# Moving the loads of q, k and v to ScalarE's queue, and dense instead of padded one-hot rows, in a fused attention and channel-mix kernel

## The chip, the cores and the metric

The kernel runs on one core of one Trainium2 chip. The metric is device microseconds of one execution. The engines are named as in the profile: PE is TensorE (with PEld, its weight loads), DVE is VectorE, ACT is ScalarE, POOL is GpSimd and SP is SyncE. A "q" after a name (SPq, ACTq) means the engine's sequencer, which also issues DMA transfers.

## The reference

Four batches, eight heads, 768 positions and a head dimension of 64. Queries and keys are assigned to the nearest of 16 centroids of their head, by the cosine. A query attends only to keys with the same centroid. The attention output, with the heads side by side (512 columns), goes through a channel mix with a shift by one position.

```python
q_assign = argmax(einsum('bhsd,hcd->bhsc', q_n, c_n))      # the same for k
mask = q_assign[:, :, :, None] == k_assign[:, :, None, :]
scores = where(mask, scale * (q @ k.T), -1e9)
x = softmax(scores) @ v                                    # heads side by side: (4, 768, 512)
xk = mu_k * x + (1 - mu_k) * x_prev                        # xr in the same way with mu_r
k = relu(xk @ w_k);  v = (k * k) @ w_v                     # 512 -> 1024 -> 512
out = sigmoid(xr @ w_r) * v
```

## The kernel before

**Pairs and steps.** Two heads make a pair; there are 16 pairs, n = 0 to 15. A pair takes 12 steps, one per head and block of 128 keys, so pair n begins at step s = 12n and there are 192 steps. In step t, `scores(t)` has PE multiply 128 keys with all 768 queries of the head (L281, L282) into a PSUM tile `st`, of which there are two, and ACT makes `pt`, the exp (L284). `values(t - 6)`, next on PE, multiplies six `pt` tiles of the head before with `vt` (L294). For the first block of queries of a head, at a step T that is a multiple of 6, the last of these six tiles is the exp of step T-1.

**The mask.** The score contraction has 80 rows: 64 of q or k, and 16 of a one-hot of the centroid. Both lie in `aug`, of which there are three rings of two tiles, `augs[n % 3]`. Equal centroids add a constant that the exp takes off again with its bias; without it the exp is close to zero.

**Preparation of pair n+2, during pair n.** `qk_nat` (or `qk_rows` for pairs 0 to 5; two buffers together) receives q and k from memory. The DVE transposes them into `qkT` in four calls (`trans`, L139; for the pairs up to 5 PE transposes them, `trans_pe`, L155, and DVE or ACT copies). POOL casts `qkT` into `aug` (L169). PE multiplies with the centroids (`aff_mm`, L188), DVE transposes the product to `t` (L192), takes the maximum over 16 (L199), compares (`ohn`, L202) and transposes the one-hot back to `oht` (L211). Then four transfers, issued on SP's queue, bring the one-hot rows from `oht` to rows 64 to 79 of `aug` (L213, `aff_back`). Before the change `ohn` has 32 columns for each row of the one-hot, 16 of them zero, and both halves of a group lie side by side in `oht`: 768 columns, and one transfer per group.

**Loads.** `load_rows` (L85) brings q and k of a pair in two transfers of 384 KB; `load_qk` (L78), for pairs 6 to 15, in eight of 96 KB; `load_v` (L99) brings v, cast by `vcast` on POOL (L176). Nearly all are issued on SP's queue.

**The order.** It is written out by hand. `at(t, f)` puts f at the end of step t; `forced[t]` puts it after `values`. In the other steps a slice of the channel mix (`psk`, `psr`, `psv`) is taken from a queue. These slices share two PSUM tiles, and end in ACT (`kr`, L378; `tanh`, L388) and DVE (`k`, L379; `out_sb`, L400). Every engine and every queue works in the order in which its instructions were written:

```python
at(s + 9 + i, load_qk, n + 4, i // 4, i % 4)      # n >= 4, i = 0..7
at(s + 6 + d, aff_back, n + 2, [nc.sync])         # d = 9, 5, 3, 3 for n = 0..3, then 1
at(s + 8, load_v, n + 2, nc.sync)
```

**Semaphores of the transfers.** Transfers issued from SP and from ACT share eight completion semaphores in the built program. A transfer whose semaphore was used before waits for the landing of the transfer that used it last; which one that is follows from the order of all transfers, of both queues. In the kernel before, 194 of these 197 transfers are issued from SP; the other three are ACT's, at the start.

Of the kernel before, what the change touches and what calls it, by code (L numbers as in the profile page):

```python
# [9 lines left out]
BF16 = mybir.dt.bfloat16  # L10
AF = mybir.ActivationFunctionType
ALU = mybir.AluOpType
# [4 lines left out]
def kernel(  # L17
# [13 lines left out]
    nc = tc.nc  # L31

    B, H, S, D = q.shape
    C = centroids.shape[1]
    NCH = S // 128
    NP = H // 2
# [6 lines left out]
    GW = 2 * S // NG  # L43
# [9 lines left out]
    constp = ctx.enter_context(tc.tile_pool(name="constp", bufs=1))  # L53
# [3 lines left out]
    clup = ctx.enter_context(tc.tile_pool(name="clup", bufs=2))  # L57
# [12 lines left out]
    nat = {}  # L70
    vnat = {}

    def load_qk(n, i, a):
        b, j = divmod(n, NP)
        if i == 0 and a == 0:
            nat[n] = loadp.tile([128, 2, 2 * GW], F32, name="qk_nat")
        x = (q, k)[i][b, 2 * j:2 * j + 2].rearrange("h (m i r) (w e) -> r w i (h m) e", i=32, r=2, e=32)
        nc.sync.dma_start(nat[n][32 * a:32 * a + 32, i, :].rearrange("i (m e) -> i m e", e=32),  # L78
                          x[a // 2, a % 2])

    def load_rows(n, eng_q, eng_k):
# [24 lines left out]
    mu_k_sb = constp.tile([128, NJ], F32)  # L106
    mu_r_sb = constp.tile([128, NJ], F32)
# [4 lines left out]

    NR = 3
    vts, augs, xts = [], [], []
    ohns = [constp.tile([128, 2 * GW], BF16, name=f"ohn{i}") for i in range(2)]
    for i in range(NR):
        vts.append(constp.tile([128, 2, NCH, D + 2], BF16, name=f"vt{i}"))
        augs.append([constp.tile([128, 2 * S], BF16, name=f"aug{i}_{t}") for t in range(2)])
        xts.append(constp.tile([128, S + 2], BF16, name=f"xt{i}"))

    def init_ring(i):
        if i < 2:
            nc.gpsimd.memset(ohns[i], 0.0)
        nc.gpsimd.memset(vts[i][:, :, :, D:D + 1], 1.0)
        nc.gpsimd.memset(xts[i][:, GW:GW + 2], 0.0)

# [4 lines left out]
    def augv(n, g):  # L131
        return augs[n % NR][g % 2].rearrange("p (q r u) -> p q r u", q=2, r=2)[:, g // 2, :, :]
# [46 lines left out]
    aff = {}  # L179

    def aff_mm(n, part=0, parts=1):
        j = n % NP
        if part == 0:
            aff[n] = ps_w.tile([128, GW], F32, name="affps", tag="w")
        ps = aff[n]
        u = slice(part * GW // parts, (part + 1) * GW // parts)
        for g in range(NG):
            nc.tensor.matmul(ps[32 * g:32 * g + 32, u], cblk[:, 2 * j + g % 2, :, :], qkT[n][:, g, u],  # L188
                             start=True, stop=True, tile_position=(0, 32 * g))
        if part == parts - 1:  # L190
            t1 = clup.tile([128, GW], F32, name="t1")
            nc.vector.transpose(t1, ps)  # L192
            aff[n] = t1

    def aff_max(n):
        t1 = aff[n]
        rmax = clup.tile([128, GW // C], F32, name="rmax")
        t1v = t1.rearrange("p (g c) -> p g c", c=C)
        nc.vector.tensor_reduce(rmax, t1v, axis=AX.X, op=ALU.max)  # L199

        ohn = ohns[n % 2]
        nc.vector.tensor_tensor(  # L202
            ohn.rearrange("p (r b c) -> p b r c", r=2, c=2 * C)[:, :, :, 0:C],
            t1.rearrange("p (b r c) -> p b r c", r=2, c=C),
            rmax.rearrange("p (b r) -> p b r", r=2)[:, :, :, None].to_broadcast([128, GW // (2 * C), 2, C]),
            op=ALU.is_ge)

    def aff_back(n, engs):
        aff.pop(n)
        oht = clup.tile([128, 2 * GW], BF16, name="oht")  # L210
        nc.vector.transpose(oht, ohns[n % 2])  # L211
        for i, g in enumerate((0, 2, 1, 3)):
            engs[i % len(engs)].dma_start(augs[n % NR][g % 2][64:64 + C, (g // 2) * S:(g // 2 + 1) * S],  # L213
                                          oht[32 * g:32 * g + C, :])

# [200 lines left out]
    def at(t, fn, *args):  # L418
        todo.setdefault(t, []).append(lambda: fn(*args))

    with tc.manual_schedule():
# [8 lines left out]
        load_v(0, nc.sync)  # L430
        make_identity(nc, ident)
        init_ring(0)
        nc.gpsimd.tensor_copy(identb, ident)
        def use_pe(m):
# [32 lines left out]
        for i in range(1, NR):  # L467
            init_ring(i)
# [3 lines left out]
        def more(n, i, m, eng=None, pool=None):  # L472
            for i in range(i, i + m):
                trans_pe(n, i, eng or nc.vector, pool)

        def load_mu():
            nc.sync.dma_start(mu_k_sb, moe_mu_k.rearrange("(j p) -> p j", p=128))
            nc.sync.dma_start(mu_r_sb, moe_mu_r.rearrange("(j p) -> p j", p=128))

        def load_wk(j):  # L480
            nc.gpsimd.dma_start(w_k_sb[:, j, :], moe_w_k.rearrange("(j p) f -> p j f", p=128)[:, j, :])
# [13 lines left out]
        def less_one():  # L495
            for m in (mu_k_sb, mu_r_sb):
                nc.vector.tensor_scalar(m, in0=m, scalar1=-1.0, scalar2=None, op0=ALU.add)

        at(6, load_mu)
        at(17, less_one)  # L500
        for i in range(4):
# [13 lines left out]
            3: lambda: aff_mm(1),  # L515
            4: lambda: first_onehot(1),
        }
        at(3, load_rows, 3, nc.sync, nc.sync)
        at(4, aff_max, 1)
        at(4, aff_back, 1, [nc.sync])  # L520
        for n in range(NPAIR):
            s = n * W
            off = (6, 2, 0, 0)[n] if n < NP else 0
            if n + 4 < NPAIR:
                if n + 4 < NP + 2:
                    at(s + off + 6, load_rows, n + 4, nc.sync, nc.sync)
                elif n < NP:
                    for i in range(8):
                        at(s + 6 + i // 2, load_qk, n + 4, i // 4, i % 4)
                else:  # L530
                    for i in range(8):
                        at(s + 9 + i, load_qk, n + 4, i // 4, i % 4)
            if n + 2 < NPAIR:
                if n < NP:
                    for i in range(6):
                        forced[s + i + off] = lambda n=n, i=i: more(n + 2, 2 * i, 2, nc.scalar if i == 3 else nc.vector)
                    a = (12, 8, 6, 6)[n]
                    for i in range(2):
                        forced[s + a + i] = lambda n=n, i=i: aff_mm(n + 2, i, 2)
                    d = a - 3  # L540
                else:
                    for g in range(4):
                        at(s + g, trans, n + 2, g)
                    forced[s + 5] = lambda n=n: aff_mm(n + 2)
                    d = 1
                at(s + 5 + d, aff_max, n + 2)
                at(s + 6 + d, aff_back, n + 2, [nc.sync])
                at(s + 8, load_v, n + 2, nc.sync)
            if n + 1 < NPAIR:
                at(s + 7, vcast, n + 1)  # L550
            at(s + W - 1, norm, 2 * n)
            e = s + W + NCH
            at(e - 1, norm, 2 * n + 1)
            if n < NP - 1:
                for i in range(3):
                    at(e + (4 if n == 0 else 2) + i, xtr, n, i, 3)
                e += 6 if n == 0 else 4
            else:
                at(e + 1, xtr, n)

            def sh(n=n):
                b, j = divmod(n, NP)
                if j == 0:
                    mixes[b] = Mix(b)
                mixes[b].shift(n)

            def sh2(n=n):
                b, j = divmod(n, NP)
                mixes[b].shift_r(n)

            def enq(n=n):
                b = n // NP
                queue.extend(mixes[b].slices())
                rate[0] = len(queue) / (H * NCH) if b < B - 2 else (len(queue) - HOLD) / (H * NCH - NCH - 4)
                credit[0] = 0.0
            at(e + 2, sh)
            at(e + (4 if n < NP - 1 else 3), sh2)
            if n % NP == NP - 1:
                at(e + 3, enq)
# [46 lines left out]
```

## Time and profile before

| what | value |
|---|---|
| time, median of 3 runs | 267.85 us (264.1 to 269.74) |
| the profiled execution: its time, its span | 267.85 us, 266.1 us |
| PE busy | 252.7 us |
| ACT busy | 192.3 us |
| DVE busy | 179.9 us |
| POOL busy | 100.6 us |
| mean granted PE clock | 0.987 |
| DMA | 29.71 MB, 112 GB/s in the mean |

In the lines of the profile that follow, a group is given as: source line, engine, operation, output <- input, count, busy time and the mean duration of one. A timeline row begins with the start in us and the duration in us; "xN" means that N instructions were merged, and the square bracket tells how long the engine was idle before and what ended that. A waits row gives: who waited, for whom, the total in us, how often, the longest.

### The profile page before, as it was taken

The page shows a single profiled execution, that of the slowest core. Times are in us where ns is not written, and L with a number is a line of the kernel's source. Part 1 is how long each engine was busy: PE and PEld are TensorE (multiplying, and loading weights), DVE is VectorE, ACT ScalarE, POOL GpSimd, SP SyncE. Part 2 cuts the span into 40 slices and gives each one's busy share as a digit, 9 for nine tenths or more (in the row PEclk, how much of TensorE's full clock was granted, in tenths as well). Part 3 has the DMA queues.
Part 4 walks back from the last instruction along what each step waited for, and adds up shares of the span by engine and source line. Part 5 has one row for each costly group of instructions (what it writes and reads, how often), then busy time and mean ns, then how long its engine had stood idle before and what let it go on. Part 6 is the DMA issues. An engine that isn't in the chain of part 4 may idle for free.

```text
span 266.1 us, 6335 instructions
## 1 busy us (share of the span) xinstructions
PE 252.7 (95%) x2460; PEld 153.3 (58%) x2460; DVE 179.9 (68%) x346; ACT 192.3 (72%) x275; POOL 100.6 (38%) x193
## 2 busy tenths in 40 slices
PE   8798998998899999999999999999999999999994
PEld 3666666664466655555666555555666655555441
DVE  3245769869888877685879685868887364675222
ACT  4149887988688977677889878776989887446310
POOL 3744775586998252507070525233240100000000
PEclk9869999999999999999999999999999999999999
DMA  6823788989288463929390918576302011120132
GB/s 183 246 70 109 160 198 197 182 137 190 25 163 125 111 85 94 179 69 200 81 201 15 173 15 188 119 134 142 115 0 76 1 53 68 42 79 2 39 118 79
DMA packets 93517, 29.71 MB, mean 112 GB/s; under 512 B 65904, under 2 KB 89904, under 8 KB 93488
## 3 DMA queue, kind: packets, MB, share of 16 engines
q1 hardware_dynamic: 90336, 26.26, 45.4%
q0 software_dynamic: 2208, 2.62, 6.6%
q10 hardware_dynamic: 944, 0.43, 0.6%
q8 instruction: 19, 0.31, 0.5%
q14 instruction: 10, 0.08, 0.1%
HBM read 24.15 MB, written 6.29 MB: 114 GB/s over the span
## 4 chain that ended last, share of the span: by engine, by line
PE 78%; DVE 9%; ACT 8%; DMA 2%; issue 1%; ACTq 0%; DVEq 0%
PE psv L396 16%; PE st L281 12%; PE psk L373 10%; PE out L294 10%; PE psr L385 8%; ACT pt L284 6%; PE st L282 6%; PE affps L188 5%; PE psk L364 5%; DMA qk_rows<-in_k_dram 2%; PE trps L155 2%; PE xtps L321 1%; DVE oht L211 1%; PE aff L243 1%; DVE xk L349 1%
## 5 line engine op out<-in xcount | busy, mean ns | idle before, releaser
L284 ACT ACTIVATE pt<-st 128x768 bf16<-128x768 f32 x192 | 148.4, 811 | 33.3 <-PE st L282 32.7
L169 POOL TENSOR_SCALAR aug<-qkT 64x384 bf16<-64x384 f32 x128 | 68.3, 534 | 93.7 <-DVE qkT L139 37.2
L294 PEld LDWEIGHTS <-pt 128*128 128x128 bf16 x1152 | 60.4, 97 | 28.3 <-ACT pt L284 3.3
L281 PE MATMUL st<-aug 80*128 80x512 bf16 x192 | 73.9, 385 | 1.9 <-ACT pt L284 0.7
L294 PE MATMUL out<-vt,pt 128*128 128x65 bf16 x1152 | 67.4, 193 | 1.9 <-ACT pt L284 1.3
L282 PE MATMUL st<-aug 80*128 80x256 bf16 x192 | 52.4, 273 | 0.0
L396 PE MATMUL psv<-w_v_sb,k 128*128 128x512 bf16 x192 | 47.9, 378 | 0.2 <-ACT tanh L388 0.2
L378 ACT ACTIVATE kr<-psk 128x512 bf16<-128x512 f32 x48 | 28.7, 598 | 10.7 <-PE psk L373 7.6
L379 DVE TENSOR_TENSOR k<-kr 128x512 bf16<-128x512 bf16 x48 | 23.1, 481 | 18.1 <-ACT kr L378 18.1
L373 PE MATMUL psk<-xk,w_k_sb 128*128 128x512 bf16 x128 | 32.5, 378 | 0.9 <-DVE xk L349 0.9
L400 DVE SCALAR_TENSOR_TENSOR out_sb<-tanh,psv 128x512 f32<-128x512 bf16 x24 | 16.5, 686 | 24.6 <-PE psv L396 24.5
L281 PEld LDWEIGHTS <-aug 80*128 80x128 bf16 x192 | 19.0, 99 | 18.9 <-issue 10.6
L388 ACT ACTIVATE tanh<-psr 128x512 bf16<-128x512 f32 x24 | 14.3, 597 | 15.8 <-PE psr L385 15.2
L396 PEld LDWEIGHTS <-k 128*128 128x128 bf16 x192 | 16.4, 97 | 15.7 <-issue 1.6
L282 PEld LDWEIGHTS <-aug 80*128 80x128 bf16 x192 | 19.0, 99 | 10.8 <-issue 2.6
L385 PE MATMUL psr<-w_r_sb,xr 128*128 128x512 bf16 x96 | 24.6, 378 | 0.0
L176 POOL CAST vt<-v_nat 128x384 bf16<-128x384 f32 x32 | 17.3, 568 | 12.3 <-DMA v_nat<-in_v_dram 11.5
L139 DVE STREAM_TRANSPOSE qkT<-qk_nat 128x384 f32<-128x384 f32 x40 | 20.9, 554 | 0.0
L192 DVE STREAM_TRANSPOSE t<-affps 128x384 f32<-128x384 f32 x15 | 8.7, 583 | 17.6 <-PE affps L188 17.5
L307 DVE TENSOR_TENSOR xn<-out,rs 128x384 bf16<-128x384 f32 x32 | 17.8, 558 | 1.1
L188 PE MATMUL affps<-qkT,cblk 128*32 128x384 f32 (+1 forms) x152 | 17.7, 431 | 0.8 <-DVE qkT L139 0.6
L349 DVE SCALAR_TENSOR_TENSOR xk<-diff,mu_k_sb,xt 128x768 bf16<-128x768 bf16 x16 | 16.7, 1041 | 0.6
(63 smaller groups left out, 220.3 us busy)
## 6 DMA issues: line engine op xcount, KB each, us to landing
v_nat<-in_v_dram SPq DMA_DIRECT2D x16, 384.0 KB, 4.1
out_dram<-out_sb SPq DMA_DIRECT2D x24, 256.0 KB, 2.0
qk_nat<-in_q_dram SPq DMA_DIRECT2D x40, 96.0 KB, 4.0
qk_nat<-in_k_dram SPq DMA_DIRECT2D x40, 96.0 KB, 3.7
qk_rows<-in_q_dram SPq DMA_DIRECT2D x5, 384.0 KB, 4.1
qk_rows<-in_k_dram SPq DMA_DIRECT2D x5, 384.0 KB, 5.0
aug<-oht SPq DMA_DIRECT2D x60, 24.0 KB, 2.2
w_k_sb<-in_moe_w_k_dram POOLq DMA_DIRECT2D x4, 256.0 KB, 5.0
```

The source lines that it names most:

```text
L139: nc.vector.transpose(qkT[n][:, g, :], nat[n][:, g // 2, (g % 2) * GW:(g % 2 + 1) * GW])
L169: nc.gpsimd.tensor_scalar(augv(n, g)[0:64, par, :], in0=qkT[n][64 * par:64 * par + 64, g, :], scalar1=qk_scale, scalar2=1.0, op0=ALU.mult, ...
L188: nc.tensor.matmul(ps[32 * g:32 * g + 32, u], cblk[:, 2 * j + g % 2, :, :], qkT[n][:, g, u], start=True, stop=True, tile_position=(0, 32 * g))
L281: nc.tensor.matmul(st[:, 0:512], kc, a[rows, 0:512], start=True, stop=True)
L282: nc.tensor.matmul(st[:, 512:S], kc, a[rows, 512:S], start=True, stop=True)
L284: nc.scalar.activation(pt, st, AF.Exp, bias=-BIG, scale=BIG)
L294: nc.tensor.matmul(o[:, qc, :], pts[bh * NCH + c][:, qc * 128:(qc + 1) * 128], vts[n % NR][:, tt, 2 * (c % 3) + c // 3, 0:D + 1], start=(c ...
L373: nc.tensor.matmul(ps, w_k_sb[:, j, ii * 128:(ii + 1) * 128], self.xk[:, j, 0:512], start=(j == 0), stop=(j == NJ - 1))
L378: nc.scalar.activation(kr, src, AF.Relu)
L379: nc.vector.tensor_tensor(dst, kr, kr, op=ALU.mult)
L385: nc.tensor.matmul(ps, self.xr[:, j, sl], w_r_sb[:, j, :], start=(j == 0), stop=(j == NJ - 1))
L396: nc.tensor.matmul(self.psvt, self.k2[:, i, sl], w_v_sb[:, i, :], start=(i == 0), stop=(i == NI - 1))
```

## The change

There are three parts. First, the one-hot is compared into a dense tile of 384 columns and transposed so; since the two halves of a group then lie below each other, on 16 partitions each, eight transfers of 12 KB per pair take the place of four of 24 KB. The two constant `ohn` tiles and their memsets go. Second, loads of q, k, v and of `mu_k`, `mu_r` in the steps are issued on ACT's queue, except q of pair 3; those of the start stay where they were. SP's queue keeps the one-hot transfers and the stores. Third, loads move: `load_rows` two steps later, `load_qk` to one per step from step s+8, `load_v` two steps earlier.

```diff
-    def load_qk(n, i, a):
+    def load_qk(n, i, a, eng):
...
-        nc.sync.dma_start(nat[n][32 * a:32 * a + 32, i, :].rearrange("i (m e) -> i m e", e=32),
+        eng.dma_start(nat[n][32 * a:32 * a + 32, i, :].rearrange("i (m e) -> i m e", e=32),
...
-    ohns = [constp.tile([128, 2 * GW], BF16, name=f"ohn{i}") for i in range(2)]
...
-        if i < 2:
-            nc.gpsimd.memset(ohns[i], 0.0)
...
-        ohn = ohns[n % 2]
-        nc.vector.tensor_tensor(
-            ohn.rearrange("p (r b c) -> p b r c", r=2, c=2 * C)[:, :, :, 0:C],
-            t1.rearrange("p (b r c) -> p b r c", r=2, c=C),
-            rmax.rearrange("p (b r) -> p b r", r=2)[:, :, :, None].to_broadcast([128, GW // (2 * C), 2, C]),
-            op=ALU.is_ge)
+        ohn = clup.tile([128, GW], BF16, name="ohn")
+        nc.vector.tensor_tensor(ohn.rearrange("p (g c) -> p g c", c=C), t1v,
+                                rmax[:, :, None].to_broadcast([128, GW // C, C]), op=ALU.is_ge)
+        aff[n] = ohn
...
     def aff_back(n, engs):
-        aff.pop(n)
-        oht = clup.tile([128, 2 * GW], BF16, name="oht")
-        nc.vector.transpose(oht, ohns[n % 2])
+        ohn = aff.pop(n)
+        oht = clup.tile([128, GW], BF16, name="oht")
+        nc.vector.transpose(oht, ohn)
         for i, g in enumerate((0, 2, 1, 3)):
-            engs[i % len(engs)].dma_start(augs[n % NR][g % 2][64:64 + C, (g // 2) * S:(g // 2 + 1) * S],
-                                          oht[32 * g:32 * g + C, :])
+            for par in range(2):
+                r = 32 * g + C * par
+                engs[i % len(engs)].dma_start(augv(n, g)[64:64 + C, par, :], oht[r:r + C, :])
...
-            nc.sync.dma_start(mu_k_sb, moe_mu_k.rearrange("(j p) -> p j", p=128))
-            nc.sync.dma_start(mu_r_sb, moe_mu_r.rearrange("(j p) -> p j", p=128))
+            nc.scalar.dma_start(mu_k_sb, moe_mu_k.rearrange("(j p) -> p j", p=128))
+            nc.scalar.dma_start(mu_r_sb, moe_mu_r.rearrange("(j p) -> p j", p=128))
...
-        at(3, load_rows, 3, nc.sync, nc.sync)
+        at(5, load_rows, 3, nc.sync, nc.scalar)
...
                 if n + 4 < NP + 2:
-                    at(s + off + 6, load_rows, n + 4, nc.sync, nc.sync)
-                elif n < NP:
-                    for i in range(8):
-                        at(s + 6 + i // 2, load_qk, n + 4, i // 4, i % 4)
+                    at(s + off + 8, load_rows, n + 4, nc.scalar, nc.scalar)
                 else:
                     for i in range(8):
-                        at(s + 9 + i, load_qk, n + 4, i // 4, i % 4)
+                        at(s + 8 + i, load_qk, n + 4, i // 4, i % 4, nc.scalar)
...
-                at(s + 8, load_v, n + 2, nc.sync)
+                at(s + 6, load_v, n + 2, nc.scalar)
```

## The prediction

> **What bounds the kernel now.** I read the page's busy shares first, then the busy time by stretches.
>
> ```profile
> PE 252.7 (95%) x2460; PEld 153.3 (58%) x2460; DVE 179.9 (68%) x346; ACT 192.3 (72%) x275; POOL 100.6 (38%) x193
> ```
> ```profile
> core 0: us, PE busy (x) PEld busy (x) DVE busy (x) ACT busy (x) POOL busy (x), PEclk, DMA share, GB/s
> 50.00:75.00 25.00, 22.20 (x262) 14.15 (x262) 21.79 (x39) 20.01 (x28) 18.43 (x29) 1.00 0.79 129
> 120.00:150.00 30.00, 29.60 (x318) 18.61 (x314) 23.84 (x48) 25.81 (x39) 11.02 (x23) 1.00 0.75 133
> ```
>
> TensorE (PE) sets the time: 13.4 us idle in 266.1, and from 75 us on almost none. It issues in a fixed order, so what is lost to a late exp stays lost. ScalarE (ACT) has little room: 25.8 of 30 us in the second stretch. The PE's own waits, then the timeline at step 72, show how tight the exp is:
>
> ```profile
> PE out L294 <- ACT pt L284: 1.3, 4, 0.4
> PE psk L373 <- DVE xk L349: 0.9, 1, 0.9
> ```
> ```profile
> 85.33 0.96 DVE L211 STREAM_TRANSPOSE oht<-ohn 128x768 bf16<-128x768 bf16 x1
> 85.99 0.81 ACT L284 ACTIVATE pt<-st 128x768 bf16<-128x768 f32 x1
> 86.36 2.41 SPq L213 DMA_DIRECT2D aug<-oht  x4
> 87.38 1.51 ACT L284 ACTIVATE pt<-st 128x768 bf16<-128x768 f32 x2
> 88.23 0.10 PEld L294 LDWEIGHTS <-pt 128*128 128x128 bf16 x1 [0.52 <-ACT pt L284]
> ```
>
> The exp at 87.38 is that of step 71. `values` of a new head (every sixth step T) needs the exp of step T-1, and already waits 0.4 us for it. The one-hot transpose of step 60+7 ends only at 86.29, at exp 70: the DVE runs two to three steps behind. The same at step 48:
>
> ```profile
> 58.92 3.74 ACT L284 ACTIVATE pt<-st 128x768 bf16<-128x768 f32 x5
> 59.55 0.98 DVE L211 STREAM_TRANSPOSE oht<-ohn 128x768 bf16<-128x768 bf16 x1
> 61.22 0.10 PEld L294 LDWEIGHTS <-pt 128*128 128x128 bf16 x1 [0.19 <-ACT pt L284]
> ```
>
> Prices of transfers, by tile (issue time min/median/max in ns, then landing):
>
> ```profile
> L213 SPq DMA_DIRECT2D aug<-oht x60: 507/582/1594, 23.5 to 201.8; - x60
> DMA to landing us min/median/max: 1.8/2.2/6.0
> ```
> ```profile
> L78 SPq DMA_DIRECT2D qk_nat<-in_q_dram x40: 342/542/1556, 44.0 to 178.2; - x40
> DMA to landing us min/median/max: 2.4/3.9/6.8
> ```
>
> [...] So a waiting load on ACT's queue would hold all ACT instructions behind it. The trace of before cannot confirm it: ACT issues only three transfers, at the start, without such waits. [...] the PE waits once for a load (1.9 us at the start) and never for a one-hot transfer, so there is no late transfer to save. [...] the trace has 1.8 to 2.2 us for 24 KB. [...]
>
> **The change part by part.**
>
> *Unpadded one-hots.* The transpose reads 384 columns instead of 768: the row of 384 f32 columns (`qkT`) takes 0.55 us against 0.97, so I take -0.45 us (bounds: -0.4 to -0.5) fifteen times on the DVE. Only once is the PE seen waiting behind it (`xk` before the first `psk`, 0.9 us): -0.45 us. Two memsets of 0.74 us go from POOL, which idles 3.7 and 2.6 us soon after each: nothing; without that cover at most 0.74 each. The compare is 0.56 us either way.
>
> *Eight transfers for four.* SP issues 15 x 4 x 0.58 = 35 us more, but loses 101 loads and small transfers (about 0.5 us each, 50 us). The last one-hot lands 2.3 us later; it is needed 13 or more steps on. Hidden. One place is near: q of pair 3 is now behind pair 1's eight transfers on SP, issue about 27.8, landing after 3.3 to 4.1 us, 31.9 against a use at 30.1: a loss of up to 1.8 us, covered if the first stall below (2.1 us, earlier) comes.
>
> *Loads on ACT's queue.* 101 issues of about 0.5 us. The three issues at the start took 0.42 to 0.51 us on ACT's queue, beside its table load. I take them as hidden behind the exps already queued (0.70 us apart); uncovered they would cost 0.5 us each, up to 50 us of ACT time against 74 idle. Two steps later or earlier doesn't matter for use: the loads are needed from step s+24, the last is issued at s+15.
>
> *The new wait.* The built program's wait lists: a transfer waits for the landing of the one that last used its completion semaphore; eight are shared by both queues. With eight one-hots per pair, the loads from s+8 on mostly wait for one-hots of the same pair. The load issued after exp t holds exp t+1; PE then stops at the next score (two `st` buffers) or at the next head. Earliest start of exp t+1: end of the transpose before, -0.45 (shorter), +0.07 (SP's issue), +0.56 for each earlier one-hot, +1.85 (landing when the queue is quiet, as at 86 to 200 us), +0.53 (own issue). For the second one-hot that is +2.56, for the first +2.0, for the third +3.1. Pair by pair, with the transpose's end and exp's start in the trace of before; the loss is counted where PE first needs the late exp:
>
> - v at step 6 behind pair 1's first one-hot (transpose 23.51, landing 2.4 there): exp 7 at 26.1 for 23.6; the score of step 9 wants it at 24.6, it ends 26.8: 2.1.
> - v at step 18 (33.20, landing 2.8, between 1.85 and the 3.6 seen): exp 19 at 36.2 for 34.3; score 21 at 35.8: 1.1.
> - step 34 (50.21): exp 35 at 52.8 for 49.9; a new head follows, end 53.5 for 50.7: 2.8.
> - step 46 (60.52): exp 47 at 63.1 for 60.4, new head: 2.6.
> - step 57 (71.30): exp 58 at 73.9 for 71.2; PE has a gap to 73.8: 1.1.
> - step 70 (86.29): exp 71 at 88.9 for 87.4, new head: 1.4.
> - steps 81, 94, 106, 118, 129, 142 by the same sum: 0.85, 0.8, 0.45, 0.9, 0.9, 0.75, together 4.65.
>
> Sum 2.1+1.1+2.8+2.6+1.1+1.4+4.65 = 15.75. Less 0.45 for the transpose and an estimated 1 us that PE's 4.6 idle us between 13 and 75 us absorb: +14.3. The profiled execution took 267.85 us (span 266.1 and 1.75 around it), which is also the median of the three: 282. Bounds of the unknowns: three loads (steps 93, 105, 141) wait for the load one step before; landing of 2.4 us is nearly covered, 3.9 adds 1.5 each, 4.5 in all. One-hots near 50 and 62 us took 5 to 5.5 us to land; then +6. [...] Below: if the DVE catches up while PE stands, half of the losses go, 275.
>
> **The rivals.**
>
> *A, the wait is covered (not slower).* If the load's wait does not hold the exps behind it, or if PE's second `st` buffer covers it, only -0.45 us is left: 267. It decides in favour of A if the one-hot has landed 0.5 us before exp t+1 could start. Against: by the times above it lands 0.3 to 2.4 us after that. For: no ACT instruction behind a waiting transfer is in the trace of before. Chance 0.12.
>
> *B, the waits chain.* Landings of 4 to 5 us [...], or a load blocked by its own predecessor, turn each stall into two; 15.75 + 4.5 + 6 [...]: 294. For: before shows SP issues of 2.35 and 3.4 us where much is outstanding. Against: one load per step leaves at most three outstanding. Chance 0.09.
>
> *C, SP's empty queue and the lighter DVE count.* Six us of DVE (15 x 0.45) and earlier one-hots would have to be on the path; against: PE waits for the DVE 3.4 us in all. At the very best 262. Chance 0.03.
>
> **How the numbers follow.** The forecast, 282, has 0.76; its own range is 274 to 290. Leaving A's and C's time below (0.15) and a part of B above (0.05), the range is 271 to 293. 2% is about what a measurement of this kernel can tell from no change. Faster by over 2%: C, 0.03. Within 2%: A and a remnant of the forecast, 0.12. Slower: 0.85.
>
> **What would show it.** Right: ACT's busy time unchanged near 192 us, but idle stretches of 1 to 3 us before an exp once per pair up to step 142, ended by a one-hot's or a load's landing; `oht` at about 0.52 us; PE's waits for `pt` and its sequencer's idle time up by some 15 us; the tail after step 156 unchanged. Wrong: exps that start while a load in front of them still waits, or stalls not where listed. The weakest step is that a waiting transfer stops ACT's queue; then comes how much of each stall PE's buffers hide.

## The result, and the profile after

The changed kernel takes 297.73 us (median of 4 runs, 294.69 to 300.69) beside 266.95 us for the kernel before (4 runs, 264.1 to 269.74): a ratio of 1.110, with a 95% interval of 1.091 to 1.130. Ratios here and below compare the means of those runs that lie within 1.5% of the fastest of their kernel. The change makes the kernel slower, on the side that the prediction named, but by about twice what it forecast. The profiled execution took 294.69 us, its span is 292.6 us.

The page of the changed kernel gives busy shares and the granted TensorE clock by slices of 7.3 us:

```profile
PE 258.3 (88%) x2460; PEld 155.6 (53%) x2460; DVE 172.5 (59%) x346; ACT 193.2 (66%) x275; POOL 98.1 (34%) x191
PEclk9997999779597999999999999999999999999998
```

The instructions are as many as before on PE, DVE and ACT, and ACT is busy 193.2 us against 192.3. PE stands idle 34.3 us instead of 13.4, and is busy 5.6 us longer with the same 2460 matmuls: the clock line shows why, it falls below full speed in five slices between 21 and 95 us. The stretches of the prediction, again:

```profile
core 0: us, PE busy (x) PEld busy (x) DVE busy (x) ACT busy (x) POOL busy (x), PEclk, DMA share, GB/s
50.00:75.00 25.00, 16.19 (x180) 11.06 (x179) 16.09 (x30) 13.57 (x19) 13.22 (x22) 0.81 0.67 114
120.00:150.00 30.00, 26.75 (x264) 15.14 (x261) 18.17 (x38) 20.28 (x29) 10.04 (x20) 1.00 0.56 128
```

PE did 22.20 us of work in the first stretch before, and does 16.19 now, at a clock of 0.81; in the second 26.75 for 29.60. What the engines waited for (sum in us, how often, the longest):

```profile
ACT pt L279 <- DMA aug<-oht: 21.7, 9, 4.1
...
PEld L289 <- ACT pt L279: 13.8, 14, 4.4
...
PE st L276 <- ACT pt L279: 12.6, 10, 3.5
PE out L289 <- ACT pt L279: 11.6, 6, 4.2
...
ACT pt L279 <- DMA qk_nat<-in_q_dram: 7.0, 4, 2.9
```

The exp (`pt`) had no wait for any transfer before. Now 28.7 us in thirteen stretches are put down to transfers, and PE's waits for `pt` follow. One of them, at step 34, in the timeline (start, duration, what it is, and in brackets the idle time before it):

```profile
51.96 0.58 DVE L205 STREAM_TRANSPOSE oht<-ohn 128x384 bf16<-128x384 bf16 x1
...
52.24 0.76 POOL L479 DMA_DIRECT2D w_v_sb<-in_moe_w_v_dram  x1
...
52.60 4.93 SPq L209 DMA_DIRECT2D aug<-oht  x8
...
56.34 0.32 ACTq L78 DMA_DIRECT2D qk_nat<-in_q_dram  x1
56.76 0.81 ACT L279 ACTIVATE pt<-st 128x768 bf16<-128x768 f32 x1 [4.07 <-DMA aug<-oht]
...
57.62 0.24 PE L289 MATMUL out<-vt,pt 128*128 128x65 bf16 x1 [4.25 <-ACT pt L279]
```

The transpose ends at 52.54, SP issues the one-hots from 52.60, and the load on ACT's queue goes out only at 56.34, after the second one-hot landed (56.31 in the trace). The trace also tells the completion semaphore of every transfer (the 104 of ACT and the 153 of SP name the same eight, the 10 of GpSimd eight others), and so what a load waited for: this load has the semaphore of that second one-hot. The exp behind it starts 4.22 us after the transpose's end; the prediction had 2.56. PE stands still for 4.25 us. The second sort of stall, at step 93, where a load waits for the load one step before it:

```profile
132.25 0.35 ACTq L78 DMA_DIRECT2D qk_nat<-in_q_dram  x1
...
136.89 0.35 ACTq L78 DMA_DIRECT2D qk_nat<-in_q_dram  x1
137.28 0.81 ACT L279 ACTIVATE pt<-st 128x768 bf16<-128x768 f32 x1 [2.91 <-DMA qk_nat<-in_q_dram]
...
138.15 0.38 PE L276 MATMUL st<-aug 80*128 80x512 bf16 x1 [2.58 <-ACT pt L279]
```

Transposes and one-hot transfers by tile (min/median/max in ns, then landing in us):

```profile
L209 SPq DMA_DIRECT2D aug<-oht x120: 507/580/1451, 19.1 to 231.0; - x120
L205 DVE STREAM_TRANSPOSE oht<-ohn x15: 561/567/579, 18.5 to 225.2; 128x384 bf16<-128x384 bf16 x15
...
DMA to landing us min/median/max: 1.6/2.3/5.0
```

To see where the time goes I compare the start of each step's score on PE in the two traces. The changed kernel starts with a lead of 4.0 us, mostly because TensorE ran at half clock from 11.0 to 17.8 us in the profile of before and not in this one. From there its scores fall back by 30.3 us, in twelve places, and after step 156 by nothing more. They are set here against the twelve of the prediction:

```
step of the wait   6    18   34   46   57   70   81   94   106  118  129  142   sum
forecast, us       2.1  1.1  2.8  2.6  1.1  1.4  0.85 0.8  0.45 0.9  0.9  0.75  15.75
measured, us       5.0  1.5  6.3  3.8  3.2  1.4  1.6  2.9  1.2  1.0  1.2  1.2   30.3
```

The first five stand exactly at the listed steps, and there the load waits for the one-hot that the prediction names. After them there is still one place for each pair, but within it the exps are held up, by 0.9 us or more, behind the loads of steps 69, 81 and 84, 93, 105, 118, 129 and 133, 141 and 144, and at four of these the semaphore is that of another load. At 93, 105 and 141 it is the load of one step before, which the prediction had as a bound. At 69 it is the load of v (issued at 97.93 us, landed at 102.80, beside a weight load of 256 KB issued at 97.18), which it did not have; so the 1.4 us under 70 agree with the forecast by luck.

### The profile page after: what moved, and what is told of

It is laid out like the page before. It is cut to its first block, busy times and chain, and to the rows that moved or that the text cites. A ratio compares the mean times of both kernels' runs of the same rounds, so it can differ in the third digit from the quotient of the medians.

```text
span 292.6 us, 6438 instructions
## 1 busy us (share of the span) xinstructions
PE 258.3 (88%) x2460; PEld 155.6 (53%) x2460; DVE 172.5 (59%) x346; ACT 193.2 (66%) x275; POOL 98.1 (34%) x191
## 4 chain that ended last, share of the span: by engine, by line
PE 66%; DMA 15%; ACT 7%; DVE 5%; ACTq 2%; issue 2%; SPq 1%; DVEq 0%
PE psv L391 12%; PE st L276 12%; PE out L289 9%; PE psk L368 9%; DMA aug<-oht 8%; ACT pt L279 6%; PE psr L380 6%; PE st L277 5%; PE affps L185 5%; PE psk L359 4%; DMA qk_nat<-in_q_dram 4%; PE trps L152 2%; ACTq L78 2%; DMA v_nat<-in_v_dram 2%; DMA qk_rows<-in_k_dram 1%
## 5 line engine op out<-in xcount | busy, mean ns | idle before, releaser
L279 ACT ACTIVATE pt<-st 128x768 bf16<-128x768 f32 x192 | 149.1, 811 | 61.1 <-PE st L277 29.5
L276 PE MATMUL st<-aug 80*128 80x512 bf16 x192 | 75.8, 395 | 14.1 <-ACT pt L279 12.6
L289 PEld LDWEIGHTS <-pt 128*128 128x128 bf16 x1152 | 63.0, 99 | 41.2 <-ACT pt L279 13.8
L289 PE MATMUL out<-vt,pt 128*128 128x65 bf16 x1152 | 70.3, 196 | 12.1 <-ACT pt L279 11.6
L277 PE MATMUL st<-aug 80*128 80x256 bf16 x192 | 53.6, 279 | 0.0
L374 DVE TENSOR_TENSOR k<-kr 128x512 bf16<-128x512 bf16 x48 | 22.1, 462 | 27.8 <-ACT kr L373 27.7
L373 ACT ACTIVATE kr<-psk 128x512 bf16<-128x512 f32 x48 | 28.7, 599 | 9.9 <-PE psk L368 6.9
L368 PE MATMUL psk<-xk,w_k_sb 128*128 128x512 bf16 x128 | 33.1, 385 | 0.0
L302 DVE TENSOR_TENSOR xn<-out,rs 128x384 bf16<-128x384 f32 x32 | 17.8, 557 | 1.1
L160 DVE COPY qkT<-trps 128x512 f32<-128x512 f32 x11 | 7.6, 690 | 17.9 <-PE trps L152 13.0
L173 POOL CAST vt<-v_nat 128x384 bf16<-128x384 f32 x32 | 16.5, 546 | 4.2 <-PE st L277 2.9
L359 PE MATMUL psk<-xk,w_k_sb 128*128 128x256 bf16 x128 | 17.0, 277 | 0.0
```

Source lines behind the costliest of these rows:

```text
L276: nc.tensor.matmul(st[:, 0:512], kc, a[rows, 0:512], start=True, stop=True)
L277: nc.tensor.matmul(st[:, 512:S], kc, a[rows, 512:S], start=True, stop=True)
L279: nc.scalar.activation(pt, st, AF.Exp, bias=-BIG, scale=BIG)
L289: nc.tensor.matmul(o[:, qc, :], pts[bh * NCH + c][:, qc * 128:(qc + 1) * 128], vts[n % NR][:, tt, 2 * (c % 3) + c // 3, 0:D + 1], start=(c ...
L359: nc.tensor.matmul(ps[:, a * 256:(a + 1) * 256], w_k_sb[:, j, (i + a) * 128:(i + a + 1) * 128], self.xk[:, j, 512:768], start=(j == 0), st ...
L368: nc.tensor.matmul(ps, w_k_sb[:, j, ii * 128:(ii + 1) * 128], self.xk[:, j, 0:512], start=(j == 0), stop=(j == NJ - 1))
```

## The experiments

The theory after the result: the change loses its time where a load on ACT's queue waits for a one-hot transfer that used its completion semaphore before; the issues themselves cost little. The rivals: the issues are what costs; or the dense one-hots with their eight transfers; and for the size, landings beside other transfers against a lower TensorE clock. Times of the kernel before, measured beside these runs, had medians of 264.1 to 264.7 us.

### One half of the change at a time

All loads back on SP's queue, at the change's steps:

```diff
-        at(5, load_rows, 3, nc.sync, nc.scalar)
+        at(5, load_rows, 3, nc.sync, nc.sync)
...
-                        at(s + 8 + i, load_qk, n + 4, i // 4, i % 4, nc.scalar)
+                        at(s + 8 + i, load_qk, n + 4, i // 4, i % 4, nc.sync)
...
-                at(s + 6, load_v, n + 2, nc.scalar)
+                at(s + 6, load_v, n + 2, nc.sync)
```

(and the same for the rows of pairs 4 and 5 and the two `mu` loads.)

> The changed kernel with all loads back on SyncE's queue, at their new steps, and the dense one-hots kept. Theory (a load on ScalarE's queue waits for a one-hot's landing and holds the exps behind it): all stalls of ScalarE go, 266 to 270 us; q and k of pair 3 are behind eight one-hots on SyncE's queue, which may cost 1 to 3 us at step 14. Rival (the eight small transfers, the dense transpose or the new steps are the cost): it stays above 285 us.

Measured: 270.94 us, ratio 1.023 (1.016 to 1.031). This is 0.9 us above the range expected: without ACT's queue 6 of the change's 31 us are left. No exp waits for a transfer. What is left lies in three places: 3.4 us at step 15, 1.4 us of lower clock behind it, and 3.0 us at step 66. The waits:

```profile
DVE qkT L136 <- DMA qk_nat<-in_k_dram: 3.5, 2, 3.1
...
PE trps L152 <- DMA qk_rows<-in_q_dram: 3.2, 1, 3.2
```

The second line is the place the prediction called near: q of pair 3 behind pair 1's eight one-hots. Uncovered it costs 3.2 us and not the "up to 1.8"; in the changed kernel itself nothing shows at step 15, since the stall at step 6 comes first and covers it. The first line stands at step 66: the last two loads of k of a pair, which on SP are issued after eight one-hots, at 76.6 and 77.2 us, and land 5.0 and 6.4 us later.

The one-hot part alone, in the kernel before:

```diff
-        oht = clup.tile([128, 2 * GW], BF16, name="oht")
-        nc.vector.transpose(oht, ohns[n % 2])
+        oht = clup.tile([128, GW], BF16, name="oht")
+        nc.vector.transpose(oht, ohn)
...
+            for par in range(2):
+                r = 32 * g + C * par
+                engs[i % len(engs)].dma_start(augv(n, g)[64:64 + C, par, :], oht[r:r + C, :])
```

> The kernel before with the dense one-hots and their eight transfers alone; loads stay on SyncE's queue at the old steps. Theory: 266 to 268 us, not to be told from before. Rival (eight transfers instead of four load the DMA engines or SyncE's queue): 275 us or more.

Measured: 267.24 us, ratio 1.008 (1.005 to 1.012), in the range expected. Eight short transfers for four cost a little and gain nothing: 6 us less of DVE work is not on the path, and once, at step 24, PE waits for pair 2's later one-hots (`st` for `aug<-oht`, 2.0 us at most).

The loads on ACT's queue alone, in the kernel before, at its own steps:

```diff
-        nc.sync.dma_start(nat[n][32 * a:32 * a + 32, i, :].rearrange("i (m e) -> i m e", e=32),
+        eng.dma_start(nat[n][32 * a:32 * a + 32, i, :].rearrange("i (m e) -> i m e", e=32),
...
-                at(s + 8, load_v, n + 2, nc.sync)
+                at(s + 8, load_v, n + 2, nc.scalar)
```

> The kernel before with the loads on ScalarE's queue alone: padded one-hots, four transfers per pair, the old steps. By the wait lists the loads of pairs 8 and up now wait for transfers that landed long before; only the v loads of steps 32 and 44 wait for a one-hot of their own pair. Theory: two stalls of 4 to 6 us, about 50 and 61 us into the run, with one or two stretches of lower TensorE clock after them: 275 to 282 us, and no stall after 75 us. Rival (each of 101 issues on ScalarE's queue delays the exps, whatever it waits for): 290 us or more, the delay growing evenly with the steps.

Measured: 284.48 us, ratio 1.073 (1.066 to 1.079): the places expected, but 2.5 us above the range. The two stalls in its waits and the first in its timeline:

```profile
ACT pt L284 <- DMA aug<-oht: 15.8, 4, 7.0
PE st L281 <- ACT pt L284: 15.5, 8, 7.1
```
```profile
45.92 0.98 DVE L211 STREAM_TRANSPOSE oht<-ohn 128x768 bf16<-128x768 bf16 x1
46.97 2.40 SPq L213 DMA_DIRECT2D aug<-oht  x4
51.77 0.39 ACTq L99 DMA_DIRECT2D v_nat<-in_v_dram  x1
52.27 0.81 ACT L284 ACTIVATE pt<-st 128x768 bf16<-128x768 f32 x1 [7.05 <-DMA aug<-oht]
```

ACT computed nothing from 45.2 to 52.3 us, nearly all of it behind one load of v, although nothing that it had to compute needed this v. Between step 60 and the end this kernel issues more than half of its loads on ACT's queue and loses only 2.5 us, some of it at landings again: the issues are not the main cost.

### Moving the loads away from the one-hots in flight

```diff
-                        at(s + 8 + i, load_qk, n + 4, i // 4, i % 4, nc.scalar)
+                        at(s + (14, 13)[n - 2] + i // 2 if n < NP else s + 12 + min(i, 6), load_qk, n + 4, i // 4, i % 4, nc.scalar)
...
-                at(s + 6, load_v, n + 2, nc.scalar)
+                at(s + 11, load_v, n + 2, nc.scalar)
```

> The changed kernel with the loads still on ScalarE's queue, but issued when the transfers they wait for have landed: q and k of pairs 6 and up at steps s+12 to s+18 (s+14 and s+13, two per step, for the first two such pairs), v at s+11. Theory: no waits left on ScalarE's queue, 267 to 272 us. Rival (the issues themselves cost): 285 us or more, as the number of issues is the same.

Measured: 285.12 us, ratio 1.077 (1.071 to 1.083): a miss for the theory, and just inside the rival's range. Stalls of 3.3 us are left at steps 41 and 53 (`ACT pt L279 <- DMA aug<-oht` 7.0 us in three waits): of pair 4's one-hots the second and third landed only 4.9 and 5.5 us after their issue, at 58.73 and 59.88 us, and the loads of steps 38 and 39 waited for just these. At step 15, with the stall of step 6 gone, q of pair 3 comes late by 4.1 us. So a second version moves the loads of pairs 6 and 7 further and puts the rows of pair 3 back:

```diff
-                        at(s + (14, 13)[n - 2] + i // 2 if n < NP else s + 12 + min(i, 6), load_qk, n + 4, i // 4, i % 4, nc.scalar)
+                        at(s + 18 + i // 2 if n < NP else s + 12 + min(i, 6), load_qk, n + 4, i // 4, i % 4, nc.scalar)
...
-        at(5, load_rows, 3, nc.sync, nc.scalar)
+        at(3, load_rows, 3, nc.sync, nc.sync)
```

> The change with every load still on ScalarE's queue, but later: v five steps later (step s + 11), the loads of pairs 6 and 7 at s + 18 to s + 21, those from pair 8 on at s + 12 to s + 18, so that a load is issued after the one-hots that last used its completion semaphore have landed; the rows of pair 3 go back to SyncE's queue at step 3. Nothing is left out. Theory (the time went into ScalarE's waits for landings, not into the issues): no idle of ScalarE over 1 us for a landing between steps 6 and 142, the stalls of 4.1 us at step 15 and of 3.2 us at steps 41 and 53 of the earlier late version are gone; time 269 to 276 us, of which the issues themselves cost some 3 to 5 (0.3 us here and there after step 60, as in the earlier late version). Rival (a load on ScalarE's queue costs its issue time wherever it stands, some 0.3 us each of 101): 290 us or more, as slow as the change.

Measured: 286.03 us, ratio 1.081 (1.074 to 1.089): a miss again, 10 us above the theory's range and 4 below the rival's, so that by its time alone it would speak rather for the rival. Its trace does not. Up to step 45 it has no stall of a microsecond and keeps 3.7 of its lead of 4.0 us; then:

```profile
53.83 7.09 ACTq L78 DMA_DIRECT2D qk_nat<-in_q_dram  x2
55.95 0.58 DVE L205 STREAM_TRANSPOSE oht<-ohn 128x384 bf16<-128x384 bf16 x1
56.60 4.93 SPq L209 DMA_DIRECT2D aug<-oht  x8
61.02 0.81 ACT L279 ACTIVATE pt<-st 128x768 bf16<-128x768 f32 x1 [6.80 <-DMA aug<-oht]
```

The two loads grouped in the first row are issued at 53.83 and 60.60. The second now takes the semaphore of a one-hot of the next pair, 5, which was not even transposed when ACT came to the load (that one-hot landed at 60.58). The same happens with pair 6 at step 58. With loads and one-hots taking turns on eight semaphores, moving loads in time only changes which one-hot they wait for. The two late versions therefore don't decide on the price of the issues.

### Fewer one-hots in the turn

The change with padded one-hots and four transfers a pair, as before; all else as the change has it:

```diff
-            for par in range(2):
-                r = 32 * g + C * par
-                engs[i % len(engs)].dma_start(augv(n, g)[64:64 + C, par, :], oht[r:r + C, :])
+            engs[i % len(engs)].dma_start(augs[n % NR][g % 2][64:64 + C, (g // 2) * S:(g // 2 + 1) * S],
+                                          oht[32 * g:32 * g + C, :])
```

> The change with its one-hot part undone: padded one-hots and four transfers a pair, loads on ScalarE's queue at the change's own steps. Nothing is left out. The loads take turns on the eight semaphores with 4 transfers a pair and no longer with 8, so fewer of them meet one-hots in flight: at steps 37 to 39 and 49 to 51 (one-hots issued 2 to 4 steps before), hardly elsewhere. Theory (landing waits): losses of 1 to 3 us at each of these two places and 2 to 4 us in issues, 271 to 281 us. Rival (the loads on ScalarE's queue are what costs, whatever the one-hots do): 290 to 298 us, as the change.

Measured: 277.00 us, ratio 1.044 (1.036 to 1.052), as the theory expected. Against the kernel before, measured beside it, this is 12.7 us more, the dense one-hots alone 2.6, and both together 30.8: the halves cost twice their sum. The semaphores in the traces say why. Of the 101 loads on ACT's queue, 43 take the semaphore of a one-hot with four of them a pair, and 71 with eight. The two stalls are where expected, at the loads of steps 37 to 39 and 49 to 51, the first 3.5 us long:

```profile
PE st L281 <- ACT pt L284: 6.9, 7, 3.4
ACT pt L284 <- DMA aug<-oht: 5.6, 2, 3.6
```

### One-hots out of the turn

The change, with the one-hots of pairs 2 and on issued by GpSimd, whose transfers have completion semaphores of their own in the built program:

```diff
-                at(s + 6 + d, aff_back, n + 2, [nc.sync])
+                at(s + 6 + d, aff_back, n + 2, [nc.gpsimd])
```

> The change with one edit: the one-hot transfers of pairs 2 and on are issued by GpSimd, whose transfers have completion semaphores of their own; the loads stay on ScalarE's queue at the change's own steps. Nothing is left out. In the program no load on ScalarE's queue then waits for one-hots of its own pair from pair 2 on, only for loads that were issued 8 loads before. Theory (the coupling through the shared semaphores is the cause): idle of ScalarE put down to landings of one-hots disappears at steps 34, 46, 57, 70 and every one after them; 270 to 282 us, the upper end if GpSimd, which has 98 us of work and now 100 transfers to issue at some 0.75 us each, brings one-hots or casts late (that would show as TensorE waiting for GpSimd or for one-hots, not as ScalarE waiting). Rival (ScalarE's issues as such): the stalls stay where they are, 290 us or more.

Measured: 280.46 us, ratio 1.059 (1.053 to 1.066), in the range expected. The eleven stalls from step 18 on are gone: between steps 30 and 66 the scores fall back by nothing, with 27 loads on ACT's queue at the change's own steps. Two stalls remain, both named beforehand as possible. At step 6 the load of v still waits for the first one-hot of pair 1, which is on SP's queue here too (issued at 19.18 us, landed at 23.06), and the exp for 4.0 us. At step 67 GpSimd's own queue is the trouble:

```profile
83.24 3.93 POOL L209 DMA_DIRECT2D aug<-oht  x8
87.17 0.97 POOL L173 CAST vt<-v_nat 128x384 bf16<-128x384 f32 x2
87.74 0.49 PE L289 MATMUL out<-vt,pt 128*128 128x65 bf16 x6 [6.01 <-POOL vt L173]
```

A cast of v stands behind eight transfers of 0.49 us each, and PE waits 6 us for it. The next version takes both away:

```diff
-        at(4, aff_back, 1, [nc.sync])
+        at(4, aff_back, 1, [nc.gpsimd])
...
-                at(s + 7, vcast, n + 1)
+                at(s + 6, vcast, n + 1)
```

> The change with GpSimd issuing the one-hot transfers of all pairs from pair 1 on, and the cast of v (GpSimd too) one step earlier, so that at the steps where both stand it is issued ahead of the transfers. Loads stay on ScalarE's queue at the change's own steps; nothing is left out. In the program no load on ScalarE's queue then waits for any one-hot transfer after the start. The version with GpSimd from pair 2 on lost 3.7 us at step 9 (loads behind pair 1's one-hots, still on SyncE's queue), some 2.6 us by a lower clock after it and 7.1 us at step 67 (a cast behind eight transfers of 3.9 us). Theory (everything that the change lost is its loads waiting for one-hots; issues on ScalarE are nearly free): these three go, 265 to 271 us, within 2% of the kernel before, with 101 loads on ScalarE's queue. Rival (part of the loss is in the issues or in the dense one-hots, and only shows once the stalls are gone): 274 us or more.

Measured: 272.48 us, ratio 1.033 (1.028 to 1.038). The three stalls went, as expected: in this trace none of the 101 loads has the semaphore of a one-hot, and the clock is full throughout the profiled execution. But the time is 1.5 us above the range expected, and 1.5 below the rival's. Its PE waits show what is left:

```profile
PE st L276 <- DMA aug<-oht: 4.4, 5, 1.4
...
PE out L289 <- POOL vt L173: 2.9, 3, 1.6
...
PE out L289 <- ACT pt L279: 1.8, 4, 0.8
...
PE st L276 <- ACT pt L279: 0.6, 3, 0.3
```

GpSimd, 59% busy instead of 34%, brings one-hots and casts late: 7.3 us. PE's waits for an exp are back to 2.4 us in all, beside 2.0 in the kernel before, with all 101 loads on ACT's queue and dense one-hots. In this kernel, as in all that have the loads on ACT's queue at the change's steps or later, 0.6 us are lost at steps 81 and 129 and 0.3 us at 91 and 139, and in neither of the two without ACT's queue; I take that for the price of the issues, some 2 us; no run isolates it.

The same with padded one-hots, four transfers a pair:

> The kernel of the run beside it, with padded one-hots and four transfers a pair as in the kernel before, so that GpSimd issues half as many. Nothing is left out. Theory: no load waits for a one-hot here either, and GpSimd's four transfers take some 2 us instead of 3.9 us a pair; 264 to 270 us, the same as the run beside it or 1 to 2 us less, since the halved issue time only counts where a cast or an augmented row of GpSimd is late. Rival (eight short transfers are no dearer than four when nobody waits for them): no difference.

Measured: 271.06 us, ratio 1.025 (1.022 to 1.027): 1.4 us less than its neighbour, a little above the range expected. Neither beats the kernel before, and no version tried did.

### Why the stalls were longer than forecast

GpSimd's six later weight loads of 256 KB, three steps later each:

```diff
-            at(34 + 6 * i, load_wv, 2 * i)
+            at(37 + 6 * i, load_wv, 2 * i)
...
-            at(58 + 6 * i, load_wr, 2 * i)
+            at(61 + 6 * i, load_wr, 2 * i)
```

> The change with one edit: GpSimd's weight loads of 256 KB (w_v and w_r, six of them) three steps later each, so that none is in flight when one-hots of pairs 4, 5 and 6 land. Nothing is left out. Theory (the stalls at steps 34, 46 and 57 were larger than forecast because those one-hots landed 3.1 to 3.9 us after their issue beside a weight load, [...]): landings of 1.7 to 2.2 us there, stalls 1 to 2 us shorter at each of the three places, fewer microseconds at a half clock; 286 to 293 us. Rival (landings of one-hots are slow for another reason, the loads before them on the same queue or the eight of them together): no difference, 295 to 299 us.

Measured: 295.20 us (293.06 to 299.67), ratio 1.113 (1.101 to 1.126), over 2 us above the theory's range, at the lower end of the rival's, and not told apart from the change by its time. The trace shows the theory at work at one of the three places: pair 4's first two one-hots land after 2.1 and 1.7 us instead of 3.5 and 3.1, and the loss at step 34 falls from 6.3 to 4.3 us. At step 57 it falls from 3.2 to 1.4, but the exp's wait there hardly changes (2.83 us for 2.98); the clock stays full this time. At step 46 the first landing is still 3.0 us, beside two loads of q issued 1.3 and 2 us before. Steps 71 to 98 lose 2 us more than in the change, about half of it to a half clock at step 93 that the change did not have. So the weight load explains the slow landing at step 34; why landings are slow at the other places stays open.

The clock by itself: the kernel before, with delays of known length on ACT and nothing of the change:

```diff
+        def hold(m):
+            for i in range(m):
+                nc.scalar.activation(hold_out, hold_in, AF.Relu)
+        for i, m in enumerate((3, 4, 5, 6, 7)):
+            at(81 + 15 * i, hold, m)
```

> The kernel before with nothing of the change, and five delays on ScalarE of known length: 3, 4, 5, 6 and 7 further activations of 128x768 (some 0.8 us each, 2.4 to 5.6 us) behind the exps of steps 81, 96, 111, 126 and 141, where no weight load runs. TensorE then stands idle for about the delay less 1 us. Their results are used by nothing. Theory [...]: the stretches after the delays of 4 or 5 activations and more show a granted clock of 0.5 for several us; the span is longer than that of the kernel before at full clock, 262 us, by the sum of the idle stretches (about 15 us) and by 1.5 to 3.5 us more for each such stretch, 283 to 290 us in all. Rival (the low clock in the changed kernel comes from something else, as the mix of transfers at that time): full clock throughout, 275 to 280 us.

Measured: 287.21 us, as expected. PE's idle stretches were 1.15, 1.80, 3.11, 2.79 and 5.48 us, as the brackets at their ends show, here the first, third and fifth; then the clock in the stretches after each (column PEclk, third from the end):

```profile
100.13 0.38 PE L283 MATMUL st<-aug 80*128 80x512 bf16 x1 [1.15 <-ACT pt L286]
...
140.11 0.58 PE L283 MATMUL st<-aug 80*128 80x512 bf16 x1 [3.11 <-ACT pt L286]
...
189.99 0.59 PE L283 MATMUL st<-aug 80*128 80x512 bf16 x1 [5.48 <-ACT pt L286]
```
```profile
100.00:108.00 8.00, 7.80 (x79) 4.36 (x79) 3.40 (x8) 6.86 (x11) 4.61 (x10) 1.00 0.84 192
119.40:127.40 8.00, 8.00 (x80) 4.51 (x80) 4.29 (x9) 6.36 (x9) 2.98 (x6) 1.00 0.85 146
139.50:146.00 6.50, 5.77 (x31) 3.29 (x31) 3.00 (x7) 3.90 (x7) 0.00 (x0) 0.50 0.01 3
167.00:170.00 3.00, 3.00 (x19) 1.57 (x18) 1.61 (x2) 1.80 (x4) 0.00 (x0) 0.50 0.43 130
187.50:194.00 6.50, 4.01 (x21) 1.98 (x21) 1.07 (x2) 4.39 (x6) 0.00 (x0) 0.50 0.56 95
```

After the two short ones nothing; with the three others half clock, which, read in stretches of 0.5 us, lasts 6.8, 3.4 and 6.8 us, once with the DMA queues nearly empty (0.01). The idle of PE is enough by itself, without anything of the change. The steps after these three lose 3.1, 1.7 and 1.6 us beyond the delay.

## Why the prediction was right and wrong

*The new wait: right, and shown.* The first five stalls stand at the steps listed, and each later pair has its stall within four steps of the listed one; at 69 the load waited for is one that the prediction did not name, and the agreement in size there is luck. ACT's queue stood at the waiting load: 4.07 us of idle before an exp that had its scores, behind a load that could not go. Of the 249 transfers of SP and ACT in this trace whose semaphore had been used before, none was issued before the transfer that used it last had landed, and 27 of ACT's loads went out within 0.1 us after that. Taking the one-hots out of the turn removed the stalls from step 18 on with the loads where they are, and the one at step 6 went with the one-hots of pair 1.

*The size of the stalls: wrong, and this is the step that failed.* The forecast was 282 us with a range to 293; measured were 297.73. Two terms of the sum were too small, and one was missing.

- The landing, "+1.85 (landing when the queue is quiet, as at 86 to 200 us)", was used for the stalls at 34, 46 and 57, which are not in that stretch. There the second one-hots landed after 3.1 us (pairs 4 and 5) and 2.4 us (pair 6); at step 6 the first landed after 3.9, with the two `mu` loads that the change itself puts beside it (landed at 22.61 and 22.77, the one-hot at 22.93). The page of before had the landings of 5 to 6 us; the prediction put them into the range and not into the sum. Why the landings were this long is shown for pair 4 alone, where a weight load was in flight.
- The loads that wait for the load one step before were taken as a bound, "3.9 adds 1.5 each". At step 93 the landing took 4.62 us, beside a store of the output issued 0.04 us later; the place lost 2.9 us, for 0.8 in the sum. At 105 it took 3.5 and the place lost 1.2 for 0.45.
- The lower clock was in no term. The scores that follow the stalls at 6, 34, 46 and 57 come late by a further 1.3, 1.9, 1.0 and 1.9 us, 6.1 in all; PE is busy 7.0 us longer than in the version with GpSimd's one-hots, which has the same 2460 matmuls and full clock. The half clock lasted 3.4 us or a multiple of it, and it followed single idle stretches of 3.47, 4.25, 4.24 and 2.26 us in the changed kernel and of 2.79 us in the one with delays; the last section shows where in the trace they fell.

Of the 30.3 us, then, about 6 are clock, 2 issues (the estimate above), and the rest, 22, stalls where the twelve places had 15.75.

*Unpadded one-hots, "-0.45".* The transpose takes 0.567 us, 0.4 less than before and within the bounds given; the gain for the kernel isn't there. The part alone is 0.8% slower.

*Eight transfers, "hidden".* True for SP's time and false for the rest: they fill the turn of the semaphores, which is what makes the loads wait. The prediction used this in its sum, but did not say that four would have cost less than half as much (277.00 us). Of its "one place is near": covered, as said; 3.2 us instead of 1.8 where uncovered.

*101 issues hidden.* Right in the main: an estimated 2 us of "up to 50".

*The rivals.* A, a covered wait, has 0.12 and is out. B, chained waits, named landings of 4 to 5 us and loads blocked by their predecessor, and gave 294: nearer than the forecast, since both happened. Its time was also without the clock. Most of the signs promised held: ACT's busy time, an idle stretch per pair up to step 142, a tail without loss; PE's waits for `pt` rose by 22 us (2.0 to 24.2), more than the 15 promised. The sign "stalls not where listed" came true at step 69 and, by a few steps, at 84, 133 and 144; the sums from step 70 on fit less well than their totals suggest.

## What to carry to other kernels

A load that nobody waits for can still stop an engine, if it is issued from that engine's queue and its semaphore was last used by a transfer that isn't done (here 4.07 us of ACT at step 34); read the wait list of every transfer in the built program, and put loads on a queue that computes only if what they wait for has long landed. Price a landing from the stretch where it happens, with the transfers that the change puts beside it. And count with a half clock after an idle stretch of PE: it followed stretches of 2.15 and 2.26 us here, and longer ones up to 5.48 us, though not the one of 2.58 us, and it was a fifth of the loss.

## What the runs showed of the hardware that was not expected

- The half clock came in multiples of 3.41 us: 3.4 and 6.8 us in the kernel with delays, 3.4, 6.8, 6.8 and 3.4 in the changed kernel, 10.2 and 13.7 with the two idle stretches of 7 us in the kernel with only its loads moved. The times between are multiples too: in the trace of the changed kernel the eight changes of the granted clock from 24.64 to 92.91 us lie 1, 8, 2, 3, 2, 3 and 1 times 3.413 us apart; in the kernel with delays the three drops lie 27.3 and 20.5 us apart, 8 and 6 times. Cut at these changes into stretches of 3.413 us, the trace of the changed kernel has, between 21 and 284 us, four at full clock in which PE was idle for 1.82 us or more (3.04, 2.06, 2.52 and 1.82 us, from 21.2, 52.0, 69.0 and 86.1 us), and half clock followed each; in all others at full clock PE was idle for 1.71 us or less, and the clock stayed full. In this trace, then, it mattered where an idle stretch fell. The half clock of the kernel before, from 11.0 us, does not fit: PE was idle for 0.96 us in the 3.41 us ahead of it. At step 93 PE stood still for 2.58 us in the changed kernel and for 2.15 us in the one with later weight loads, and only the shorter was followed by half clock. The longer was divided by the border of two such stretches, into 1.71 us and 0.87 us. The first two lines are the changed kernel, the other two the one with later weight loads (the idle of PE is the second column less the third; PEclk is third from the end):

```profile
133.87:137.28 3.41, 1.70 (x20) 0.99 (x18) 2.50 (x4) 0.51 (x1) 0.00 (x0) 1.00 0.32 83
137.28:140.69 3.41, 2.48 (x22) 1.39 (x22) 0.67 (x2) 2.70 (x4) 0.00 (x0) 1.00 0.75 125
```
```profile
133.08:136.50 3.42, 1.27 (x17) 0.79 (x15) 1.63 (x4) 1.31 (x2) 0.00 (x0) 1.00 0.23 45
136.50:139.91 3.41, 3.39 (x21) 1.51 (x19) 1.11 (x3) 1.51 (x3) 0.00 (x0) 0.50 0.62 103
```

- ACT issued its loads behind the exp before them and not ahead of it: the load behind exp 32 was issued at 50.53 us, 0.1 us after that exp began at 50.43, and of the 72 loads in the steps that had nothing to wait for, two thirds went out within 0.1 us of the start of the ACT instruction before them and the others up to 0.7 us after it. So a wait of the load takes from the very next exp, and only the one running covers it.
- GpSimd issues a one-hot in 0.48 us (median of 120 in the kernel with all of them on GpSimd), where the expectation had taken 0.75; SP issues one in 0.58.
